# The first pair of heads in larger pieces, turned by TensorE, in a hash-attention and feed-forward kernel

## The chip, the cores and the metric

The kernel runs on one core of a Trainium2 chip. Times are device microseconds (us) of one execution. The granted clock is the share of its full clock that TensorE was allowed at a time. PE is TensorE's matmuls, PEld its weight loads, DVE VectorE, ACT ScalarE, POOL GpSimd and SP SyncE. A "q" behind an engine's name is that engine's instruction queue, which also issues transfers.

## The reference

```python
# q, k, v: (4, 8, 768, 64); proj: (64, 6); w_in: (512, 2048); w_out: (2048, 512); fp32
q_bits = einsum(q, proj) > 0;  k_bits = einsum(k, proj) > 0     # 6 bits per row
mask   = bucket(q_bits) == bucket(k_bits)
attn   = softmax(where(mask, q k^T / 8, -1e9)) @ v
x      = attn as (3072, 512)
h      = x @ w_in
out    = (h * sigmoid(1.702 h)) @ w_out
```

The weights arrive in 64-bit form and have to be converted to fp32 on the chip.

## The kernel before

Heads are worked on two at a time, so there are 16 pairs, numbered 0 to 15. A pair has four groups of products on TensorE: scores of three key tiles against half of the queries, then the product with v of the group before. The hash bits enter the scores as one more small product, so equal buckets need no mask. For each pair, k and q are loaded in 32 x 32 blocks and turned by VectorE, hashed by TensorE, compared by VectorE into a tile `f`, and eight small copies bring the rows of `f` to the partitions where the bits are needed:

```python
def hashed(n):
    h = dots[n] = mps.tile([P, HS], F32, tag="m", name="hash")
    for i, x in enumerate("kq"):
        for c in range(2):
            r0 = D * i + 32 * c
            nc.tensor.matmul(h[r0 : r0 + 32, :], pf[x], xts[n, x][:, c * HS : (c + 1) * HS], ...)

def featured(n, queues):
    f = wk.tile([P, HS], BF16, tag="f", name="f", bufs=1)
    nc.vector.tensor_scalar(f, dots.pop(n), above[:, 0:1], weight[:, 0:1], op0=Alu.is_gt, op1=Alu.mult)
    for c in range(2):
        for i, x in enumerate("kq"):
            for j in range(2):
                queues[j].dma_start(out=feats[n % 2][x][...], in_=f[...])      # eight row copies
```

Between these, VectorE converts w_in piece by piece: 12 of its 16 pieces during attention, and four (`LATE = 4`) in the feed-forward part, where product 4 needs sums made from the last of them. The main loop, cut to what the change touches:

```python
fetch(0, "k"); fetch(0, "q", (nc.scalar, nc.gpsimd)); fetch_v(0)
for x in "kq": turn(0, x); measure(0, x); fetch(1, x)
hashed(0); featured(0, (nc.sync, nc.scalar)); begin(0, nc.scalar)
for g in range(len(groups) + 4):                  # groups of pair n, at = 0..3
    scores(n, c, range(kt, kt + GT), g > 0)
    if 4 <= g and groups[g - 4][2]: invert(*groups[g - 4][:2])     # 1 / column sums
    if n < last and at < 2: turn(n + 1, "kq"[at]); measure(n + 1, "kq"[at])
    ...
    if n < last and at == 1:
        hashed(n + 1); featured(n + 1, (nc.sync, nc.sync))
        fetch(n + 2, "k"); fetch(n + 2, "q"); fetch_v(n + 1)
    if 3 <= g ...: total(*groups[g - 3][:2])      # column sums by TensorE ("dn")
    ...                                           # conversion steps at at = 0, 2, 3
```

At the very end stands a branch to code that would redo the work in a safe form. With this data that code never runs.

Of the kernel before, what the change touches and what calls it, by code (L numbers as in the profile page):

```python
# [19 lines left out]
P = 128  # L20
# [18 lines left out]
def kernel(  # L39
# [38 lines left out]
    pb = const.tile([P, P], F32, name="pb")  # L78
    nc.vector.memset(pb, 0.0)
    for j in range(2):  # L80
        nc.scalar.dma_start(out=pb[D * j : D * (j + 1), D * j : D * j + NB], in_=proj)
# [21 lines left out]
    for i, (x, signs) in enumerate((("k", (-1.0, 1.0)), ("q", (1.0, -1.0)))):  # L103
        w = pf[x] = const.tile([P, 32], F32, name=f"pf_{x}")
        nc.vector.memset(w, 0.0)
        nc.vector.memset(weight[D * i : D * (i + 1)], FEAT[x])
        for j in range(2):
            rows = slice(D * j, D * (j + 1))
            for h, sign in enumerate(signs):
                c0 = NB * (2 * j + h)  # L110
                nc.vector.tensor_scalar(w[rows, c0 : c0 + NB], pb[rows, D * j : D * j + NB], sign, None, op0=Alu.mult)
        for c in range(2):
            r0 = D * i + 32 * c
            for f in reversed(range(4)):
                nc.vector.memset(above[r0 : r0 + NB * (f + 1)], 0.0 if signs[f % 2] > 0 else -NORMAL)

# [52 lines left out]
    LATE = 4  # L169
# [43 lines left out]
    def prepare(wk, mps, tiles, scale, out_of):  # L213
# [31 lines left out]
    def attention(ff):  # L245
# [4 lines left out]
        with actx:  # L250
# [22 lines left out]
            def fetch(n, name, queues=(nc.sync, nc.sync)):  # L273

                b, hp = pairs[n]
                x = raws[n, name] = ld.tile([P, S // 32, 32], F32, tag=name, name=name)
                src = {"k": k, "q": q}[name]
                for j in range(2):
                    rows = src[b, 2 * hp + j].rearrange("(s p) (a i) -> a p s i", p=32, i=32)
                    for a in range(D // 32):  # L280
                        r0 = D * j + 32 * a
                        queues[j].dma_start(out=x[r0 : r0 + 32], in_=rows[a])

            def fetch_v(n):
                b, hp = pairs[n]
                x = vts[n] = ld.tile([P, T, 2, D], F32, tag="v", name="v", bufs=2)
                for j in range(2):
                    nc.sync.dma_start(out=x[:, :, j, :], in_=v[b, 2 * hp + j].rearrange("(t p) d -> p t d", p=P))
# [24 lines left out]
            def featured(n, queues):  # L313
                f = wk.tile([P, HS], BF16, tag="f", name="f", bufs=1)
                nc.vector.tensor_scalar(f, dots.pop(n), above[:, 0:1], weight[:, 0:1], op0=Alu.is_gt, op1=Alu.mult)
                for c in range(2):
                    for i, x in enumerate("kq"):
                        for j in range(2):
                            r0 = D * i + 32 * c + 2 * NB * j
                            queues[j].dma_start(out=feats[n % 2][x][D * j : D * j + 2 * NB, c * HS : (c + 1) * HS],  # L320
                                                in_=f[r0 : r0 + 2 * NB, :])

            def scores(n, c, kts, bits_first):
                qT, kT, qf, kf = xts[n, "q"], xts[n, "k"], feats[n % 2]["q"], feats[n % 2]["k"]
                cols = slice(c * HS, (c + 1) * HS)
                ps = [sps.tile([P, 2, 512], F32, tag="s", name="ps") for _ in kts]

                dot, bits = (kT, qT), (kf, qf)
                todo = [(p, kt, x) for x in ((bits, dot),) for p, kt in zip(ps, kts)] if bits_first else \
                    [(p, kt, (x,)) for x in (dot, bits) for p, kt in zip(ps, kts)]  # L330
                for p, kt, xs in todo:
                    keys = slice(kt * P, (kt + 1) * P)
                    for x in xs:
                        for j in range(2):
                            hs = slice(D * j, D * (j + 1))
                            first = x is (bits if bits_first else dot)
                            nc.tensor.matmul(p[:, j, 0:HS], x[0][hs, keys], x[1][hs, cols], start=first, stop=not first)  # L337
                for p, kt in zip(ps, kts):
                    nc.scalar.activation(es[c][:, kt, :, 0:HS], p[:, :, 0:HS], Act.Exp, scale=1.0 / D**0.5)  # L339
# [65 lines left out]
            def begin(n, *args):  # L405
                if n < min(len(in_chunks) - LATE, last + 1):
                    conv[n] = convert(cv, *in_chunks[n], *args)
# [13 lines left out]
            fetch(0, "k")  # L421
            fetch(0, "q", (nc.scalar, nc.gpsimd))
            fetch_v(0)
            for x in "kq":
                turn(0, x)
                measure(0, x)
                if last:
                    fetch(1, x)
            hashed(0)
            featured(0, (nc.sync, nc.scalar))  # L430
            begin(0, nc.scalar)
            for g in range(len(groups) + 4):
                n, c, kt = groups[g] if g < len(groups) else (last + 1, 0, 0)
                at = 2 * c + kt // GT
                if n <= last:
                    scores(n, c, range(kt, kt + GT), g > 0)
                if 4 <= g and groups[g - 4][2]:
                    invert(*groups[g - 4][:2])
                if n < last and at < 2:
                    turn(n + 1, "kq"[at])  # L440
                    measure(n + 1, "kq"[at])
                if 4 <= g and groups[g - 4][2]:
                    norm(*groups[g - 4][:2])
# [5 lines left out]
                if n < last and at == 1:  # L449
                    hashed(n + 1)  # L450
                    featured(n + 1, (nc.sync, nc.sync))
# [4 lines left out]
                if 3 <= g <= len(groups) + 2 and groups[g - 3][2]:  # L456
                    total(*groups[g - 3][:2])
                if n == last and at in (1, 3):
                    guard(at // 2)
                if at == 0:  # L460
                    step(n)
                elif at == 2:
                    step(n, 2)
                    if n > last - len(x_sums):
                        x_sums[n - last - 1]()
# [3 lines left out]
                if g == len(groups):  # L469
                    for f in in_sums(0):  # L470
                        f()
                    early.close()
# [3 lines left out]
    def shifted_attention():  # L476
# [3 lines left out]
        with actx:  # L480
# [48 lines left out]

            for n, (b, hp) in enumerate(pairs):  # L530
                tiles, ready = load(ld, n, 1), {}
                for f in prepare(wk, mps, tiles, -1.0 / D**0.5, ready):
# [14 lines left out]
    def feed_forward(tag, late=()):  # L547
# [4 lines left out]
        with ExitStack() as fctx:  # L552
# [105 lines left out]
            for sb in range(n1):  # L658
                for mt in range(FC // 2):
                    n = sb * (FC // 2) + mt  # L660
                    if n == 1:
# [7 lines left out]
                        todo += [lambda: [next(steps) for _ in range(2 * LATE // 2)]] * 2 if late else []  # L669
# [74 lines left out]
```

## Time and profile before

| | before |
|---|---|
| time, median of 6 runs with the result | 945.08 us (944.55 to 945.32) |
| span of the profile | 943.7 us |
| PE busy | 916.0 us, 97% |
| PE waits before 22 us | 15.4 us |
| PE waits at the passage to the feed-forward part | 1.4 and 2.5 us |
| end of the last vector operation to the end of the span | 7.5 us |

With an engine at 97%, the busy shares say only that little can be won. The list of what that engine waits for says where. The prediction below shows the lines.

### The profile page before, as it was taken

To read this page: it belongs to the slowest core of one execution; us is meant where nothing else is said; L and a number is where in the kernel's file an instruction comes from. 1 tells how busy PE (TensorE), PEld (TensorE's weight loads), DVE (VectorE), ACT (ScalarE), POOL (GpSimd) and SP (SyncE) were. 2 spreads that over 40 slices of the span, in tenths; PEclk is the share of its full clock that TensorE was granted. 3 is DMA by queue.
4 is the path that set the end of the run, shared out by engine and by line. 5 is a ranking of instruction groups with operands and counts; after the bars stand their busy time and mean duration, and the time that the engine had idled before them with its cause. 6 is when DMAs were issued, how large, how long until landed. Compare 5 with 4: busy or idle time off the path is not lost.

```text
span 943.7 us, 11414 instructions
## 1 busy us (share of the span) xinstructions
PE 916.0 (97%) x4193; PEld 527.6 (56%) x4193; DVE 566.8 (60%) x785; ACT 300.2 (32%) x481; POOL 160.9 (17%) x114
## 2 busy tenths in 40 slices
PE   3999999999999999989999999999999999999996
PEld 1444444444444444434444444447888888888885
DVE  3689999899877655797877787435222313141410
ACT  1666666666666642223233323221000000000000
POOL 2422332332243361050001000500000000000000
PEclk9999999999999999999999999999999999999999
DMA  8434345443333101343333383228242415130101
GB/s 119 82 78 80 78 85 103 96 92 80 77 56 66 39 23 73 128 156 135 133 134 131 124 305 132 90 89 267 93 131 74 149 62 162 56 123 12 34 11 37
DMA packets 177185, 94.30 MB, mean 100 GB/s; under 512 B 128416, under 2 KB 160672, under 8 KB 177120
## 3 DMA queue, kind: packets, MB, share of 16 engines
q1 hardware_dynamic: 175056, 92.53, 34.9%
q10 hardware_dynamic: 1968, 0.76, 0.4%
q8 instruction: 35, 0.57, 0.3%
q0 software_dynamic: 96, 0.20, 0.1%
q14 instruction: 30, 0.25, 0.1%
HBM read 60.82 MB, written 31.46 MB: 98 GB/s over the span
## 4 chain that ended last, share of the span: by engine, by line
PE 56%; DVE 1%; DMA 0%; POOL 0%; issue 0%; DVEq 0%; SPq 0%
PE product L638 31%; PE product L596 25%; DMA raw<-in_moe_w_in_dram 0%; DVE w_in_sb L156 0%; DVE bits L149 0%; DVE c L580 0%; DVE sign L152 0%; DVE sign L146 0%; POOL s_in L173 0%; POOL w_in_sb L174 0%; DVE w_in_sb L161 0%; DVE w_in_sb L158 0%; DVE c L569 0%; DVE bits L147 0%; POOL s_in L175 0%
## 5 line engine op out<-in xcount | busy, mean ns | idle before, releaser
L339 ACT ACTIVATE e<-ps 128x768 f32<-128x768 f32 x192 | 153.3, 812 | 99.4 <-PE ps L337 97.7
L337 PE MATMUL ps<-qT,kT 64*128 64x384 f32 x768 | 157.4, 490 | 0.0
L362 PE MATMUL av<-e,v 128*64 128x385 f32 x768 | 138.4, 495 | 0.0
L596 PE MATMUL product<-xT,w_in_sb 128*128 128x512 f32 x288 | 135.6, 593 | 0.0
L600 ACT ACTIVATE c<-c 128x512 f32<-128x512 f32 x72 | 45.2, 630 | 174.5 <-DVE c L571 126.2
L567 ACT COPY u<-product 128x512 f32<-128x512 f32 x30 | 17.3, 577 | 248.1 <-PE product L638 242.0
L596 PE MATMUL product<-t_x,s_in 128*128 128x512 f32 x192 | 92.0, 602 | 2.5 <-POOL s_in L175 2.5
L362 PEld LDWEIGHTS av<-e,v 128*64 128x64 f32 x768 | 49.3, 136 | 80.6 <-issue 79.9
L348 POOL TENSOR_TENSOR acc<-e 128x768 f32<-128x768 f32 x32 | 55.8, 1743 | 224.1 <-DVE acc L354 179.5
L596 PEld LDWEIGHTS product<-xT,w_in_sb 128*128 128x128 f32 x288 | 54.7, 191 | 69.7 <-issue 62.1
L337 PEld LDWEIGHTS ps<-qT,kT 64*128 64x128 f32 x768 | 69.6, 192 | 31.1 <-issue 31.1
L568 DVE TENSOR_TENSOR v<-product,u 128x512 f32<-128x512 f32 x30 | 20.6, 687 | 86.9 <-PE product L638 72.3
L337 PE MATMUL ps<-qf,kf 64*128 64x384 bf16 x384 | 63.8, 331 | 5.5 <-DMA qf<-f 5.3
L596 PEld LDWEIGHTS product<-t_x,s_in 128*128 128x128 f32 x192 | 36.8, 192 | 49.3 <-issue 45.5
L638 PE MATMUL product<-w_out_sb,xT 128*128 128x256 f32 x288 | 63.6, 379 | 0.0
L638 PE MATMUL product<-w_out_sb,w_in_sb 128*128 128x256 f32 x288 | 63.6, 379 | 0.0
L638 PE MATMUL product<-t_out,xT 128*128 128x256 f32 x288 | 63.6, 379 | 0.0
L638 PEld LDWEIGHTS product<-w_out_sb,xT 128*128 128x128 f32 x288 | 54.7, 190 | 7.9 <-issue 0.5
L638 PEld LDWEIGHTS product<-w_out_sb,w_in_sb 128*128 128x128 f32 x288 | 54.7, 190 | 7.4
L638 PEld LDWEIGHTS product<-t_out,xT 128*128 128x128 f32 x288 | 54.7, 190 | 7.4
L349 POOL TENSOR_TENSOR acc<-acc,e 128x768 f32<-128x768 f32 x32 | 55.1, 1721 | 2.5
L337 PEld LDWEIGHTS <-kf 64*128 64x128 bf16 x384 | 19.0, 95 | 61.3 <-issue 38.0
(104 smaller groups left out, 1108.1 us busy)
## 6 DMA issues: line engine op xcount, KB each, us to landing
g_dram<-c SPq DMA_DIRECT2D x72, 256.0 KB
xT<-g_dram SPq DMA_DIRECT2D x12, 1024.0 KB
w_in_sb<-g_dram SPq DMA_DIRECT2D x12, 1024.0 KB
raw<-in_moe_w_out_dram SPq DMA_DIRECT2D x16, 512.0 KB
raw<-in_moe_w_in_dram SPq DMA_DIRECT2D x15, 512.0 KB
k<-in_k_dram SPq DMA_DIRECT2D x64, 96.0 KB
v<-in_v_dram SPq DMA_DIRECT2D x32, 192.0 KB
g_dram<-u SPq DMA_DIRECT2D x24, 256.0 KB
```

The source lines that it names most:

```text
L337: nc.tensor.matmul(p[:, j, 0:HS], x[0][hs, keys], x[1][hs, cols], start=first, stop=not first)
L339: nc.scalar.activation(es[c][:, kt, :, 0:HS], p[:, :, 0:HS], Act.Exp, scale=1.0 / D**0.5)
L348: nc.gpsimd.tensor_tensor(acc, e[0], e[1], op=Alu.add)
L349: nc.gpsimd.tensor_tensor(acc, acc, e[2], op=Alu.add)
L362: nc.tensor.matmul(av[D * j : D * (j + 1), :], vt[:, t, j, :], es[c][:, t, j, :], start=(t == 0), stop=(t == T - 1))
L567: nc.scalar.copy(u, product(1))
L568: nc.vector.tensor_tensor(v, product(6), u, op=Alu.add)
L596: nc.tensor.matmul(ps, wq[LEFT[i]][:, kc, :], xq[RIGHT[i]][:, kc, :], start=(kc == 0), stop=(kc == K2 - 1))
L600: nc.scalar.activation(c, c, Act.Gelu_apprx_sigmoid)
L638: nc.tensor.matmul(ps[:, m, :], x[:, m * P : (m + 1) * P], wqs[RIGHT[i]][:, c, :], start=(c == 0), stop=(c == FC // 2 - 1))
```

## The change

Its intent is to start TensorE earlier. k and q of the first pair come in 256-byte packets. TensorE turns them, in six transposes each, and makes their hashes with the bits already on the rows where they are needed, so pair 0 has no row copies. The turning of pair 1 moves one group later (`turns = at - (n == 0)`). Conversion starts one pair later and runs to pair 14, so two pieces are left for the end instead of four. The last inversion moves ahead of the first vector work of the feed-forward part. The diff, cut to its core:

```diff
+            def first_pair():
+                for name, src, order, queue in (("k", k, "(p t) d -> p t d", nc.sync), ("q", q, "(t p) d -> p t d", nc.scalar)):
+                    x = ld.tile([P, T, 2, D], F32, tag=name, name=name)
+                    for j in range(2):
+                        queue.dma_start(out=x[:, :, j, :], in_=src[b, 2 * hp + j].rearrange(order, p=P))
+                for name, move in (("k", nc.vector.tensor_copy), ("q", nc.scalar.copy)):
...
+                        nc.tensor.transpose(tp[:, c, i * P : (i + 1) * P], x[:, t], ident)
+                    move(xt.rearrange("p (c s) -> p c s", c=2), tp[:, :, 0:HS])
+                for c in range(2):
+                    for name in "kq":
+                        nc.tensor.matmul(h, pf0[name]..., xts[0, name][:, cols], start=True, stop=True)
+                        nc.vector.tensor_scalar(feats[0][name][:, cols], h, above0[name][:, 0:1], FEAT[name], ...)
...
-    LATE = 4
+    LATE = 2
...
-                if n < min(len(in_chunks) - LATE, last + 1):
-                    conv[n] = convert(cv, *in_chunks[n], *args)
+                if n - 1 < len(in_chunks) - LATE:
+                    conv[n] = convert(cv, *in_chunks[n - 1], nc.sync if n > 1 else nc.scalar)
...
+                turns = at - (n == 0)
-                if n < last and at < 2:
-                    turn(n + 1, "kq"[at])
+                if n < last and 0 <= turns < 2:
+                    turn(n + 1, "kq"[turns])
...
+                elif at == 1 and n > last - len(x_sums):
+                    x_sums[n - last - 1]()
...
                 if g == len(groups):
                     for f in in_sums(0):
                         f()
+                    invert(*started[g + 1])
+                    norm(*started.pop(g + 1))
```

The products for pair 0's dot parts, which before were made ahead of the bits, now follow the bits like everybody else's.

More of the change, by code (lines that the diff above doesn't have):

```diff
@@ L75 @@
     nc.scalar.activation(const.tile([1, 1], F32, name="first"), ones[0:1, 0:1], Act.Exp)
-    pb = const.tile([P, P], F32, name="pb")
-    nc.vector.memset(pb, 0.0)
+    pj = const.tile([P, NB], F32, name="pj")
     for j in range(2):
-        nc.scalar.dma_start(out=pb[D * j : D * (j + 1), D * j : D * j + NB], in_=proj)
+        nc.scalar.dma_start(out=pj[D * j : D * (j + 1)], in_=proj)
     def offsets(name, row):
@@ L110 @@
                 c0 = NB * (2 * j + h)
-                nc.vector.tensor_scalar(w[rows, c0 : c0 + NB], pb[rows, D * j : D * j + NB], sign, None, op0=Alu.mult)
+                nc.vector.tensor_scalar(w[rows, c0 : c0 + NB], pj[rows], sign, None, op0=Alu.mult)
         for c in range(2):
@@ L115 @@
                 nc.vector.memset(above[r0 : r0 + NB * (f + 1)], 0.0 if signs[f % 2] > 0 else -NORMAL)
+    pf0 = {x: const.tile([P, 2, D], F32, name=f"pf0_{x}") for x in "kq"}
+    above0 = {x: const.tile([P, 1], F32, name=f"above0_{x}") for x in "kq"}
+    for i, x in enumerate("kq"):
+        nc.gpsimd.memset(pf0[x], 0.0)
+        nc.gpsimd.memset(above0[x], 0.0)
+        for j in range(2):
+            nc.gpsimd.tensor_copy(pf0[x][:, j, 0 : 2 * NB], pf[x][:, 2 * NB * j : 2 * NB * (j + 1)])
+            nc.gpsimd.tensor_copy(above0[x][D * j : D * j + 2 * NB], above[D * i : D * i + 2 * NB])
     xT = const.tile([P, KC, N], F32, name="xT")
@@ L211, in load, with prepare @@
         return tiles
-    def prepare(wk, mps, tiles, scale, out_of):
+    def prepare(wk, mps, pb, tiles, scale, out_of):
         steps = []
@@ L271, in attention, with fetch @@
             raws, vts, xts = {}, {}, {}
-            def fetch(n, name, queues=(nc.sync, nc.sync)):
+            def fetch(n, name):
                 b, hp = pairs[n]
@@ L281, in fetch @@
                         r0 = D * j + 32 * a
-                        queues[j].dma_start(out=x[r0 : r0 + 32], in_=rows[a])
+                        nc.sync.dma_start(out=x[r0 : r0 + 32], in_=rows[a])
             def fetch_v(n):
@@ L287, in fetch_v @@
                 for j in range(2):
-                    nc.sync.dma_start(out=x[:, :, j, :], in_=v[b, 2 * hp + j].rearrange("(t p) d -> p t d", p=P))
+                    order = "(t p) d -> p t d" if n else "(p t) d -> p t d"
+                    nc.sync.dma_start(out=x[:, :, j, :], in_=v[b, 2 * hp + j].rearrange(order, p=P))
+            def first_pair():
+                b, hp = pairs[0]
+                for name, src, order, queue in (("k", k, "(p t) d -> p t d", nc.sync), ("q", q, "(t p) d -> p t d", nc.scalar)):
+                    x = ld.tile([P, T, 2, D], F32, tag=name, name=name)
+                    raws[0, name] = x.rearrange("p t j d -> p (t j) d")
+                    for j in range(2):
+                        queue.dma_start(out=x[:, :, j, :], in_=src[b, 2 * hp + j].rearrange(order, p=P))
+                for name, move in (("k", nc.vector.tensor_copy), ("q", nc.scalar.copy)):
+                    x = raws[0, name].rearrange("p (t j) d -> p t (j d)", j=2)
+                    xt = xts[0, name] = wk.tile([P, S], F32, tag=f"{name}T", name=f"{name}T")
+                    tp = sps.tile([P, 2, 512], F32, tag="s", name="tp")
+                    for t in range(T):
+                        c, i = divmod(t, GT)
+                        nc.tensor.transpose(tp[:, c, i * P : (i + 1) * P], x[:, t], ident)
+                    move(xt.rearrange("p (c s) -> p c s", c=2), tp[:, :, 0:HS])
+                    measure(0, name)
+                for c in range(2):
+                    cols = slice(c * HS, (c + 1) * HS)
+                    for name in "kq":
+                        h = sps.tile([P, 2, 512], F32, tag="s", name="hash0")[:, 0, 0:HS]
+                        nc.tensor.matmul(h, pf0[name].rearrange("p j d -> p (j d)"), xts[0, name][:, cols], start=True, stop=True)
+                        nc.vector.tensor_scalar(feats[0][name][:, cols], h, above0[name][:, 0:1], FEAT[name],
+                                                op0=Alu.is_gt, op1=Alu.mult)
             def turn(n, name):
@@ L311, in hashed, with featured @@
                                          start=True, stop=True)
-            def featured(n, queues):
+            def featured(n):
                 f = wk.tile([P, HS], BF16, tag="f", name="f", bufs=1)
@@ L319, in featured, with scores @@
                             r0 = D * i + 32 * c + 2 * NB * j
-                            queues[j].dma_start(out=feats[n % 2][x][D * j : D * j + 2 * NB, c * HS : (c + 1) * HS],
+                            nc.sync.dma_start(out=feats[n % 2][x][D * j : D * j + 2 * NB, c * HS : (c + 1) * HS],
                                                 in_=f[r0 : r0 + 2 * NB, :])
-            def scores(n, c, kts, bits_first):
+            def scores(n, c, kts):
                 qT, kT, qf, kf = xts[n, "q"], xts[n, "k"], feats[n % 2]["q"], feats[n % 2]["k"]
                 cols = slice(c * HS, (c + 1) * HS)
-                ps = [sps.tile([P, 2, 512], F32, tag="s", name="ps") for _ in kts]
-                dot, bits = (kT, qT), (kf, qf)
-                todo = [(p, kt, x) for x in ((bits, dot),) for p, kt in zip(ps, kts)] if bits_first else \
-                    [(p, kt, (x,)) for x in (dot, bits) for p, kt in zip(ps, kts)]
-                for p, kt, xs in todo:
+                for kt in kts:
+                    ps = sps.tile([P, 2, 512], F32, tag="s", name="ps")
                     keys = slice(kt * P, (kt + 1) * P)
-                    for x in xs:
+                    for a, m, last in ((kf, qf, False), (kT, qT, True)):
                         for j in range(2):
                             hs = slice(D * j, D * (j + 1))
-                            first = x is (bits if bits_first else dot)
-                            nc.tensor.matmul(p[:, j, 0:HS], x[0][hs, keys], x[1][hs, cols], start=first, stop=not first)
-                for p, kt in zip(ps, kts):
-                    nc.scalar.activation(es[c][:, kt, :, 0:HS], p[:, :, 0:HS], Act.Exp, scale=1.0 / D**0.5)
+                            nc.tensor.matmul(ps[:, j, 0:HS], a[hs, keys], m[hs, cols], start=not last, stop=last)
+                    nc.scalar.activation(es[c][:, kt, :, 0:HS], ps[:, :, 0:HS], Act.Exp, scale=1.0 / D**0.5)
             accs, avs = {}, {}
@@ L403, in step, with begin @@
                     next(conv.get(n, iter(())), None)
-            def begin(n, *args):
-                if n < min(len(in_chunks) - LATE, last + 1):
-                    conv[n] = convert(cv, *in_chunks[n], *args)
+            def begin(n):
+                if n - 1 < len(in_chunks) - LATE:
+                    conv[n] = convert(cv, *in_chunks[n - 1], nc.sync if n > 1 else nc.scalar)
                     step(n)
@@ L419, in guard @@
                     nc.vector.tensor_reduce(largest[0:1, 0:1], row, axis=AX.X, op=Alu.max)
-            fetch(0, "k")
-            fetch(0, "q", (nc.scalar, nc.gpsimd))
+            started = {}
+            first_pair()
             fetch_v(0)
             for x in "kq":
-                turn(0, x)
-                measure(0, x)
-                if last:
-                    fetch(1, x)
-            hashed(0)
-            featured(0, (nc.sync, nc.scalar))
-            begin(0, nc.scalar)
+                fetch(1, x)
             for g in range(len(groups) + 4):
@@ L435, in attention @@
                 if n <= last:
-                    scores(n, c, range(kt, kt + GT), g > 0)
-                if 4 <= g and groups[g - 4][2]:
-                    invert(*groups[g - 4][:2])
-                if n < last and at < 2:
-                    turn(n + 1, "kq"[at])
-                    measure(n + 1, "kq"[at])
-                if 4 <= g and groups[g - 4][2]:
-                    norm(*groups[g - 4][:2])
+                    scores(n, c, range(kt, kt + GT))
+                turns = at - (n == 0)
+                if g in started:
+                    invert(*started[g])
+                if n < last and 0 <= turns < 2:
+                    turn(n + 1, "kq"[turns])
+                    measure(n + 1, "kq"[turns])
+                if g in started:
+                    norm(*started.pop(g))
                 if 1 <= g <= len(groups):
@@ L448, in attention @@
                         unload(*groups[g - 1][:2])
-                if n < last and at == 1:
+                if n < last and turns == 1:
                     hashed(n + 1)
-                    featured(n + 1, (nc.sync, nc.sync))
+                    featured(n + 1)
                     for x in "kq":
@@ L457, in attention @@
                     total(*groups[g - 3][:2])
+                    started[g + 1] = groups[g - 3][:2]
                 if n == last and at in (1, 3):
@@ L461, in attention @@
                     step(n)
+                elif at == 1 and n > last - len(x_sums):
+                    x_sums[n - last - 1]()
                 elif at == 2:
                     step(n, 2)
-                    if n > last - len(x_sums):
-                        x_sums[n - last - 1]()
                 elif at == 3:
@@ L528, in turn @@
                             nc.vector.tensor_copy(dst, tp)
+            pb = st.tile([P, P], F32, name="pb", bufs=1)
+            nc.vector.memset(pb, 0.0)
+            for j in range(2):
+                nc.vector.tensor_copy(pb[D * j : D * (j + 1), D * j : D * j + NB], pj[D * j : D * (j + 1)])
             for n, (b, hp) in enumerate(pairs):
                 tiles, ready = load(ld, n, 1), {}
-                for f in prepare(wk, mps, tiles, -1.0 / D**0.5, ready):
+                for f in prepare(wk, mps, pb, tiles, -1.0 / D**0.5, ready):
                     f()
@@ L668, in feed_forward @@
                         steps = conversions(cv, late + [(w_out_sb[:, :, fc, :], wo[fc]) for fc in range(FC)])
-                        todo += [lambda: [next(steps) for _ in range(2 * LATE // 2)]] * 2 if late else []
+                        todo += [lambda: [next(steps) for _ in range(LATE)]] * 2 if late else []
                         todo += [lambda: (next(steps), next(steps))] * FC
```

## The prediction

> **What bounds the kernel now.** I read the page first, for the busy shares:
>
> ```profile
> PE 916.0 (97%) x4193; PEld 527.6 (56%) x4193; DVE 566.8 (60%) x785; ACT 300.2 (32%) x481; POOL 160.9 (17%) x114
> ```
>
> TensorE (PE) is busy for 916.0 of 943.7 us. A change that leaves its matmuls alone can only win from the other 27.7 us, or from matmuls that run slowly. So the next view is the list of PE's waits:
>
> ```profile
> PE hash L310 <- DVE kT L293: 7.7, 1, 7.7
> PE ps L337 <- DMA qf<-f: 5.3, 1, 5.3
> PE product L596 <- POOL s_in L175: 2.5, 1, 2.5
> PE hash L310 <- DVE qT L293: 2.4, 1, 2.4
> PE dn L380 <- DVE rt L387: 1.4, 1, 1.4
> PE ps L337 <- ACT e L339: 0.3, 1, 0.3
> ```
>
> These are all: 19.6 us. The rest is the end: PE's last matmul ends at 935.5 and the last vector operation and store follow, about 8 us, which the change does not touch. Of the 19.6, 15.4 are before 22 us, 1.4 and 2.5 at the passage from attention to the feed-forward part. The order of time shows where:
>
> ```profile
> 7.73 1.50 PE L310 MATMUL hash<-kT,pf_k 128*32 128x384 f32 x4 [7.73 <-DVE kT L293]
> 10.62 0.98 DVE L293 STREAM_TRANSPOSE qT<-q 128x768 f32<-128x768 f32 x1 [2.94 <-DMA q<-in_q_dram]
> 13.07 3.55 PE L337 MATMUL ps<-qT,kT 64*128 64x384 f32 x12
> 21.89 1.15 PE L337 MATMUL ps<-qf,kf 64*128 64x384 bf16 x6 [5.27 <-DMA qf<-f]
> ...
> 27.18 2.16 PE L362 MATMUL av<-e,v 128*64 128x385 f32 x12
> ...
> 363.53 0.87 PE L380 MATMUL dn<-acc,ones 128*64 128x384 f32 x4 [1.36 <-DVE rt L387]
> ...
> 401.78 0.69 DVE L161 SCALAR_TENSOR_TENSOR w_in_sb<-size,w_in_sb 128x512 f32<-128x512 f32 x1
> ...
> 404.81 3.68 PE L596 MATMUL product<-t_x,s_in 128*128 128x512 f32 x4 [2.46 <-POOL s_in L175]
> 408.29 1.92 PE L596 MATMUL product<-xT,w_in_sb 128*128 128x512 f32 x4
> ```
>
> At the start: q lands at 10.6, the hashes go through VectorE and eight small copies onto their rows, and only at 21.9 can PE go on. The first value product, at 27.18, is my mark; from there PE is never idle until 362. At 404.8 PE waits for sums made from the last converted piece of w_in, whose conversion ends at 402.5.
>
> [...]after 404.81 four matmul pieces take until 408.29, 3.48 us, where the same four start 1.72 apart when warm; from 21.89 to about 26 the granted clock is 0.50.[...] 128-byte packets of k and q moved at 213 GB/s at best (2.5 to 3.0 us, 859 packets), 256-byte ones of v at 257 (61.0 to 61.5, 512 packets)[...] Here a copy of hash rows issued at 19.59 releases PE at 21.89: 2.3 us.
>
> **Part 1, the start.** k and q now come in four issues of 192 KB with 256-byte packets; none is on GpSimd's queue, whose issues took 5.2 us to land. Before, data of both queues moved about in order of issue (the scalar queue's second q piece, issued at 2.53, moved at 5.0 to 5.5, after all of k). The new order: k in two, proj, v and q interleaved, then v of the next pair. q is complete after 3 x 1536 packets at 1024 per us (512 in 0.5 us), 4.5 us from the first packet at 1.8: 6.3, say 6.6. From k's last packet to its use was 1.6 us (5.0 to 6.6), so q is there at about 8.2.
> - Six transposes. Cold weight loads take 0.34 us each (warm 0.19), so an estimated 2.4: 10.7. The copy on ScalarE (like an exp of 768, 0.81) runs beside the first hash.
> - Four hash products in a row, all ahead of the scores in PE's order. A cold pair of 32-column hashes took 1.50 for four pieces at 7.73; two pieces of 128 x 384, run alone, should take 1.28 cold, 0.64 warm. Four cold: 5.1, so 15.8; if the clock comes up on the way, 14. VectorE's evictions (0.68 each, as L315's) fit between; no copy to other rows is left. I take 15.3 for the first score.
> - Two groups of scores at 2.45 (three times 0.82 at 30 us) bring the first value product to 20.2 against 27.18. The dot products made ahead at 13.07 are lost, which this counting has inside. **Gain 7.0.**
>
> **Part 2, pair 1 shifted by one group.** Its hash moves one group closer to its use. In the trace, from the hash's end at 30.1 the fourth row copy, issued at 33.3, lands 2.3 later: 5.5 after the hash, where PE then has one group, 4.6 us. **Loss 0.9.** In the built order the last of pair 2's four pieces of k moved behind all eight row copies: issue about 7.1 after the hash, landing 2.9 later (estimate), at 10. From that turn of k to the end of the turn of q, VectorE took 7.7 us before (39.67 to 47.3), of which 1.3 was waiting beside GpSimd. The next hash is due 15.5 after, so PE waits 1 to 2. **Loss 1.3.**
>
> **Part 3, conversion one pair later, two pieces fewer at the end.** Fourteen of sixteen pieces are now converted in attention, in pairs 1 to 14, where pairs 12 to 14 had none; the four 1.22 us sums of x fall in pairs 12 to 15 too. VectorE, by stretches of 19.97 us, has 18.0 to 18.9 busy in a conversion pair; with a sum it is full. But it idles 1.1 to 1.8 us per pair for the raw piece (at 229.6 and 250.9), whose issue sits behind other loads on the queue, so the sum should fall into that gap. With a little lateness: **loss 0.6.** In the feed-forward part each of two slots converts one piece instead of two: the last one ends near 396 instead of 402.5 and its sums by 399, before PE needs them at 402.4. That frees the 2.46 and the half-clock stretch after it (3.48 - 1.72 = 1.76): **gain 4.2.**
>
> **Part 4, the last inversion.** The reciprocal of the last pair's first half now stands ahead of the feed-forward's vector work, so the second half's total finds its buffer free. **Gain 1.4**, and 0.1 of slower pieces after it.
>
> **Sum.** 7.0 - 0.9 - 1.3 - 0.6 + 4.2 + 1.5 = 9.9. 945.1 - 9.9 = 935.2, rounded 935.
>
> **Rivals.**
> 1. *The start is hidden anyway, or given back.* For: PE still starts cold and has twelve transposes more; four hashes are serial; q's landing depends on v, queued between. If q lands at 10 and all stays cold, the start gains 5, and with 3 us of stall in pair 1 the total is 6: 939. Against: 5.3 us of waiting for row copies is gone whatever the loads do.
> 2. *VectorE becomes the bound in pairs 12 to 14.* For: 18.9 of 19.97 plus 1.22. Turn of q and hash are already 0.07 us apart there (254.79, 254.85), so lateness goes straight to PE. Three pairs at 1.3 would cost 4 more than I count, also 939. Against: the raw wait.
> 3. *All fits.* Transposes warm the clock after all, the stalls of part 2 vanish in the queue's slack: first score at 13.5, no losses: 9 + 5.7 = about 14.5, 930.5.
> 4. *The late conversion was not the last thing that held product 4.* The chain of waits goes through it step by step from 388 to 404.8, so I give this little: without that gain, 939.
>
> **Range and chances.** The passage (5.7) rests on measured waits; the start (5 to 9) and the new stalls (0.5 to 5) are worked out. Both bad ends together give 940, both good 930; 8 in 10 lies in 930.5 to 939.5. Faster by over 2% needs 926.2, 18.9 us, nearly all the idle time there is before the tail: 0.03. Slower by 2% needs 19 us of new stalls in an otherwise full PE: 0.01.
>
> **What would show it.** PE's waits without s_in L175 and without rt L387; the first value product near 20; q's copy near 10.7; a wait of about 1 us for a row copy at pair 1 and one for the turn of q at pair 2; no wait of PE from 40 us to the end of attention longer than 0.5. Wrong would be: a first value product after 23, a PE wait in pairs 12 to 14 over 1 us, or a wait at product 4 that stays.

## The result, and the profile after

The changed kernel took 936.78 us (median of 6 runs, 935.9 to 937.59) against 945.08. Ratios in this document are the mean time of one kernel's fast runs over that of the other's of the same rounds, so not quite the ratio of the medians that are quoted. Here the ratio is 0.9912, interval 0.9899 to 0.9925: 8.3 us less, "within 2%", and inside the range. The predicted time was 935.0.

First the page's busy shares of the changed kernel:

```profile
PE 915.0 (98%) x4205; PEld 529.6 (57%) x4205; DVE 567.0 (61%) x786; ACT 301.8 (32%) x482; POOL 159.4 (17%) x124
```

Nothing in the amount of work moved: the twelve more TensorE instructions are the twelve transposes. The waits of PE (us in total, times, longest):

```profile
PE tp L315 <- POOL above_q L124: 7.2, 1, 7.2
PE ps L368 <- DMA qf<-f: 2.0, 1, 2.0
PE tp L315 <- DMA q<-in_q_dram: 0.5, 1, 0.5
PE hash L346 <- DVE qT L329: 0.4, 1, 0.4
```

The first is the wait for k: the name given is the semaphore that the profile dates last, but the transposes start when ScalarE starts on k, both at 7.1 us. The waits for `s_in` and for `rt` are gone. Two small ones are new, and the timeline shows them in their places (start, duration, engine, line, operation, and in brackets the idle time before it with its releaser):

```profile
9.15 1.51 PE L315 MATMUL tp<-ident,q 128*128 128x128 f32 x6 [0.48 <-DMA q<-in_q_dram]
...
10.46 1.48 PE L322 MATMUL hash<-kT,pf_k 128*128 128x384 f32 x2
11.74 1.30 PE L322 MATMUL hash<-qT,pf_q 128*128 128x384 f32 x2
12.88 0.81 PE L322 MATMUL hash<-kT,pf_k 128*128 128x384 f32 x2
13.53 0.81 PE L322 MATMUL hash<-qT,pf_q 128*128 128x384 f32 x2
...
19.21 2.16 PE L392 MATMUL av<-e,v 128*64 128x385 f32 x12
...
29.63 0.35 ACTq L144 DMA_DIRECT2D raw<-in_moe_w_in_dram  x1
...
33.42 0.40 PE L368 MATMUL ps<-qf,kf 64*128 64x384 bf16 x2 [2.02 <-DMA qf<-f]
...
34.03 0.51 SPq L291 DMA_DIRECT2D k<-in_k_dram  x1
...
43.57 0.84 PE L346 MATMUL hash<-kT,pf_k 128*32 128x384 f32 x4
44.76 0.84 PE L346 MATMUL hash<-qT,pf_q 128*32 128x384 f32 x4 [0.35 <-DVE qT L329]
...
357.61 0.87 PE L410 MATMUL dn<-acc,ones 128*64 128x384 f32 x4
...
386.85 0.69 DVE L170 SCALAR_TENSOR_TENSOR w_in_sb<-size,w_in_sb 128x512 f32<-128x512 f32 x1
...
389.11 0.73 POOL L184 TENSOR_TENSOR s_in<-s_in,w_in_sb 128x256 f32<-128x256 f32 x1
...
396.27 1.88 PE L632 MATMUL product<-t_x,s_in 128*128 128x512 f32 x4
```

Of the clock at the start, the views by stretches print 1.00, but the trace holds no record of it before 12.69 us, where the first one, of the full clock, begins. That TensorE was at half clock until then is read from the durations: the hashes of 10.46 and 11.74 start 1.28 us apart, those of 12.88 and 13.53 only 0.65.

The first value product comes at 19.21 instead of 27.18, which is 7.97 us earlier. By the first feed-forward product, 4.49 are left (349.88 against 345.39). At pair 1, PE waits 2.0 us for a row copy. At pair 2 the hashes of k and q, which stand side by side in a later pair, come one after the other. From the value product before them to the scores after them it is 4.25 us (41.28 to 45.53) instead of 2.87 (47.09 to 49.96 before), so this costs 1.4 us, of which the wait shown is 0.35. The passage to the feed-forward part gives 5.85 more: `dn` follows without a wait. The last conversion ends at 387.5 and GpSimd's sums from it at 389.8, 6.4 us before the product that needs them (396.27, the one that waited until 404.81 before). PE's last product ends 10.35 us earlier than before.

But the span is only 8.3 us shorter. From the end of the last vector operation to the end of the span it was 7.5 us before (943.7 less 936.20) and is 9.5 after (935.4 less 925.86). Apart from the last store, which has been moved by 929 us in the changed kernel, only fetches of instructions move in that time. The queue's line of the view of transfers, of the last eight or nine us (packets, MB, share), is for the kernel before:

```profile
q14 instruction: 4, 0.03, 1.8%
```

and for the changed kernel:

```profile
q14 instruction: 5, 0.04, 1.8%
```

One fetch more; five make 0.04 MB, so each is of 8 KB. The starts of SyncE's last instructions, in ns from one to the next, after its last branch, show where it falls:

```
before: 2722, 78, 64, 67, 59, 62, 59, 62, ...
after:  2766, 81, 2197, 83, 64, 66, 60, 61, ...
```

These are the semaphore waits that close the program; they start some 70 ns apart (59 to 83). In the changed kernel SyncE stands still for 2.2 us between the second and the third, from 931.98 to 934.18, and one of the five fetches, of 8192 bytes, moves in that time, from 932.70 to 933.01. In both kernels 2.7 us pass after the branch, and two of the fetches move in them (from 940.11 to 940.98 before, from 929.79 to 930.60 after). That SyncE waits for the fetch in the 2.2 us, because its closing instructions lie in two of the 8192-byte pieces, is theory, which a run below tests.

### The profile page after: what moved, and what is told of

Read it like the earlier page. It is cut to its first block, busy times and chain, and to the rows that moved or that the text cites. A ratio compares the mean times of both kernels' runs of the same rounds, so it can differ in the third digit from the quotient of the medians.

```text
span 935.4 us, 11429 instructions
## 1 busy us (share of the span) xinstructions
PE 915.0 (98%) x4205; PEld 529.6 (57%) x4205; DVE 567.0 (61%) x786; ACT 301.8 (32%) x482; POOL 159.4 (17%) x124
## 4 chain that ended last, share of the span: by engine, by line
PE 96%; DMA 1%; DVE 1%; SPq 1%; issue 0%; ACTq 0%; ACT 0%; DVEq 0%
PE product L674 31%; PE product L632 31%; PE ps L368 16%; PE av L392 14%; PE dn L410 2%; PE hash L346 1%; DMA q<-in_q_dram 1%; SPq L356 1%; PE hash L322 0%; DMA k<-in_k_dram 0%; DVE bits L156 0%; PE tp L315 0%; DVE qT L329 0%; DVE kT L329 0%; DVE acc L383 0%
## 5 line engine op out<-in xcount | busy, mean ns | idle before, releaser
L368 PE MATMUL ps<-qT,kT 64*128 64x384 f32 x768 | 155.2, 482 | 0.0
L607 DVE TENSOR_TENSOR c<-product,c 128x512 f32<-128x512 f32 x30 | 20.7, 691 | 53.6 <-PE product L674 37.3
```

The source lines that it names most:

```text
L368: nc.tensor.matmul(ps[:, j, 0:HS], a[hs, keys], m[hs, cols], start=not last, stop=last)
L607: nc.vector.tensor_tensor(c22, p, c21, op=Alu.add)
```

## The experiments

All were correct and ran for five rounds beside the kernel before, whose medians in these rounds were 944.8 to 946.3. So a difference of less than about 1 us between medians of different rounds is not settled by the times alone. Each edit is one of the changed kernel.

### The first raw piece on SyncE's queue

```diff
-                    conv[n] = convert(cv, *in_chunks[n - 1], nc.sync if n > 1 else nc.scalar)
+                    conv[n] = convert(cv, *in_chunks[n - 1], nc.sync)
```

> Only the first raw piece of w_in is issued on the sync queue (there early, before pair 1's k) instead of the scalar queue at 29.6 us, where its 512 KB moved between 30.5 and 32.9 and pair 1's row copies stood still. Theory A (the wait of 2.0 us for the row copies is all that the raw piece costs, and it adds to the rest): that wait falls to about 0.9 and the last matmul ends 1.1 us earlier than in the changed kernel. Rival B (behind it stands a second chain, row copies issued until 34.0, then the fourth piece of pair 2's k, then VectorE until the turn of q at 44.7): the first wait falls to 0.9, but the wait for the turn of q grows from 0.35 to about 1.4 and the end moves by less than 0.3 us.

The question is why the row copies of pair 1 took 2.0 us of waiting where 0.9 was predicted. In the changed kernel, from 27 to 37 us, ScalarE's queue moved the first raw piece of w_in (packets, MB, share) among the row copies:

```profile
q10 hardware_dynamic: 144, 0.52, 15.9%
```

With the raw piece early on SyncE's queue, ahead of pair 1's loads, that line is gone and the wait for rows is 0.4 us. But the time is 936.63 us (ratio 0.9905, the changed kernel's was 0.9912): nothing gained. The lines of this run say why:

```profile
43.71 0.84 PE L346 MATMUL hash<-kT,pf_k 128*32 128x384 f32 x4 [1.54 <-DVE rt L417]
44.91 0.84 PE L346 MATMUL hash<-qT,pf_q 128*32 128x384 f32 x4 [0.35 <-DVE qT L329]
```

The hash of pair 2 comes at the same place, 43.7, whether PE waits before it or at it. Its chain is the other one: the last piece of pair 2's k stands behind eight row copies on the queue (issued at 34.14 here, 34.03 in the changed kernel), then come VectorE's turn of k, its work of that group, and the turn of q. The two losses were two waits on one chain. (This profile is of the slowest of the four runs. It lost another 0.9 us at the hash of pair 14, at 291.84, where a raw piece came late to VectorE and the hash was split in the same way.)

### The shift of pair 1 undone

```diff
-                turns = at - (n == 0)
+                turns = at
```

> Only the shift of pair 1's turns, hash and row copies by one group is undone; the start, the conversion's shift and the rest stay. Theory (the shift costs 3.3 us: a wait of 2.0 for row copies and 1.2 at the next hash, and pair 1's k and q land by 17 us, early enough for the old place): both waits vanish and the last matmul ends 3.3 us earlier, about 921.9. Rival (k and q of pair 1 land too late for the old place, which is why it was shifted): a new wait of 1 to 3 us at the first hash, and no gain.

This took 934.0 us (933.81 to 934.47, ratio 0.9881), 2.8 less than the changed kernel. k and q of pair 1 are there in time (VectorE turns them at 14.5 and 16.5), and the wait for row copies is gone from PE's list. The split hash of pair 2 is still there:

```profile
40.43 0.84 PE L346 MATMUL hash<-kT,pf_k 128*32 128x384 f32 x4
41.62 0.84 PE L346 MATMUL hash<-qT,pf_q 128*32 128x384 f32 x4 [0.35 <-DVE qT L329]
```

So the shift bought nothing at the start and cost the 2.0 us. Of the 3.3 us expected, the 1.2 at the next hash did not come. PE's last product ended at 922.1, close to the 921.9 expected, only because the start, which the edit does not touch, was 0.95 us quicker in this profile.

### Also k of pair 2 ahead of the row copies

```diff
-                turns = at - (n == 0)
+                turns = at
...
+                    if n + 2 <= last:
+                        fetch(n + 2, "k")
                     featured(n + 1)
-                    for x in "kq":
-                        if n + 2 <= last:
-                            fetch(n + 2, x)
+                    if n + 2 <= last:
+                        fetch(n + 2, "q")
```

> The changed kernel with the shift of pair 1 undone (which gave 934.0 us) and all four loads of the third pair's k issued ahead of the row copies of the second. In the run with the shift undone the last two of these loads stood behind the row copies, k landed at 33.9 us and the hash of the third pair came in two parts, 1.2 us later than one. Theory: k lands before 25 us, the hash of the third pair comes in one piece, the end of the last vector operation is 1.0 to 1.3 us earlier, 932.8 us. Rival 1: the row copies are issued later behind the loads and the first score of the second pair waits for them (0.5 to 1.5 us), 934 us. Rival 2: q of the third pair, still behind the row copies, sets the time of the hash by itself, 934 us.

VectorE now turns that k at 28.47 instead of 33.89 us (it had landed by then and VectorE was held by the scores that read the tile it writes, so when it landed isn't seen), and the hash of pair 2 is one piece again, k and q side by side:

```profile
40.32 0.52 PE L346 MATMUL hash<-kT,pf_k 128*32 128x384 f32 x2
40.34 0.52 PE L346 MATMUL hash<-qT,pf_q 128*32 128x384 f32 x2
40.67 0.49 PE L346 MATMUL hash<-kT,pf_k 128*32 128x384 f32 x2
40.68 0.49 PE L346 MATMUL hash<-qT,pf_q 128*32 128x384 f32 x2
```

PE waits for nothing after q's landing. The last vector operation of the profiled run ended at 921.7 against 922.8 of the run above, 1.1 earlier, as expected. The time is 933.71 us (ratio 0.9877 against 0.9881): the times alone don't resolve it.

### Four late conversions again

```diff
-    LATE = 2
+    LATE = 4
```

> Only the number of pieces of w_in left for the feed-forward part goes back from two to four; the start and the early inversion stay. Theory: the wait for s_in and the stretch at half clock after it come back, 2.5 + 1.8 = 4.2 us, last matmul at about 929.4. Rival (part of that gain came from the shorter vector work elsewhere, or pairs 12 to 14 pay for their conversions): less than 3 us later.

939.49 us (938.98 to 941.86, ratio 0.9946), 2.7 more than the changed kernel. The wait is back:

```profile
397.93 1.98 PE L632 MATMUL product<-t_x,s_in 128*128 128x512 f32 x4 [2.31 <-POOL s_in L184]
399.75 1.88 PE L632 MATMUL product<-xT,w_in_sb 128*128 128x512 f32 x4
```

The half-clock stretch that followed it in the kernel before is not: the next four start 1.82 later, not 3.48. The two slowest of the five runs, 940.44 and 941.86, have a mean clock of 0.994 where the profiled one has 0.996, so in those the stretch may have come; no trace of them was taken. The wait cost 2.31 us in this profile, and in that of the kernel before 4.2 with the slow stretch (2.46 and 1.76).

### The last inversion back in its place

```diff
                 if g == len(groups):
                     for f in in_sums(0):
                         f()
-                    invert(*started[g + 1])
-                    norm(*started.pop(g + 1))
```

> The changed kernel with the early last inversion undone: the last column sums are inverted one task later, as before. Theory (the step of the prediction): the first vector work of the next stage waits again for the inversion, so the wait of TensorE for the first dn product, 1.4 us before the change, is back, the first feed-forward product comes 1.4 to 1.5 us later, and the kernel takes 938.2 us (the changed kernel 936.8). Rival: with the late conversion shorter the queue of VectorE is empty there anyway, no wait, 936.8 us.

937.95 us (ratio 0.9919), 1.2 more than the changed kernel by the medians and 0.7 by the ratios, close to the 938.2 expected, with the wait of before to a hundredth:

```profile
360.16 0.87 PE L410 MATMUL dn<-acc,ones 128*64 128x384 f32 x4 [1.36 <-DVE rt L417]
```

This profiled run was its slowest, 939.39 (the others 937.72 to 938.01), and shows what the wait for row copies at 34 us can do. Of the view by stretches (from and to, length, PE, PEld, DVE, ACT and POOL busy, granted clock, DMA share, GB/s), this run:

```profile
36.00:40.00 4.00, 4.00 (x21) 1.93 (x20) 2.20 (x3) 2.81 (x4) 0.00 (x0) 0.75 0.74 118
```

and the changed kernel's:

```profile
36.00:40.00 4.00, 4.00 (x28) 1.88 (x28) 2.78 (x3) 2.72 (x7) 0.00 (x0) 1.00 0.81 130
```

After a wait of 2.16 us the clock was at 0.50 from 34.58 to 37.99, so 0.75 on average here, and PE did 21 matmuls where it does 28 at the full clock. After the 2.02 us of the changed kernel it did not fall (1.00 from 33 to 40 us). Other waits went both ways too: after the 2.46 us of the kernel before, at product 4, it was at 0.50 from 404.94 to 408.36; after the 2.31 us of the run with four late conversions it stayed at 1.00 (395 to 408.3).

### Warming the clock: matmuls, and transposes

```diff
+                warm = sps.tile([P, 2, 512], F32, tag="s", name="warm")
+                for i in range(18):
+                    nc.tensor.matmul(warm[:, 0, 0:P], ident, ident, start=True, stop=True)
```

> Eighteen matmuls of the identity with itself are put ahead of the first transposes, where TensorE waits idle for k until 7.1 us; nothing else. Theory (the first hashes run at half clock because TensorE was idle): with TensorE busy from about 1.5 us on, the first two hash products take 0.64 instead of 1.3 us each and the first score starts 1 to 1.5 us earlier, the end likewise. Rival (the evictions and the arrival of q set the start, or the clock has fallen again by 9 us since the matmuls end near 7): less than 0.4 us.

```diff
+                for i in range(22):
+                    nc.tensor.transpose(warm[:, 0, 0:P], ident, ident)
```

> The changed kernel with 22 transposes of the identity on TensorE, from 1.5 us on, ahead of the first pair's turns (the earlier run with 18 matmuls there had the turns in 0.85 us and the hashes in 0.8 to 0.9 us instead of 1.51 and 1.3 to 1.5 us). Theory A: transposes do not count as work for the clock, so turns take 1.5 us, the first hash 1.5 us as in the changed kernel, first score at 14.3 us after the start. Theory B: they count like matmuls, turns 0.85 us, hashes 0.8 to 0.9 us, first score 13.0 to 13.6 us. The time of the whole kernel 936.2 to 937.2 us in either, since the run with matmuls gave the same time as the changed kernel.

Both stand ahead of the first turns. With matmuls:

```profile
9.58 0.85 PE L318 MATMUL tp<-ident,q 128*128 128x128 f32 x6 [1.06 <-DMA q<-in_q_dram]
10.26 0.81 PE L325 MATMUL hash<-kT,pf_k 128*128 128x384 f32 x2
11.40 0.88 PE L325 MATMUL hash<-qT,pf_q 128*128 128x384 f32 x2 [0.33 <-ACT qT L319]
```

With transposes:

```profile
8.77 0.85 PE L318 MATMUL tp<-ident,q 128*128 128x128 f32 x6 [1.30 <-DMA q<-in_q_dram]
9.45 0.81 PE L325 MATMUL hash<-kT,pf_k 128*128 128x384 f32 x2
10.60 0.88 PE L325 MATMUL hash<-qT,pf_q 128*128 128x384 f32 x2 [0.33 <-ACT qT L319]
```

The turns of q take 0.85 instead of 1.51 us and the first hashes 0.81 and 0.88 instead of 1.48 and 1.30, in both. The first record of the full clock begins at 5.92 us with the matmuls and at 6.09 with the transposes, when TensorE had done nothing but these transposes. So the 22 transposes brought the clock up as the 18 matmuls did. The times, 937.12 (ratio 0.9909) and 936.2 us (0.9906), are hardly different from the changed kernel's. In the profiles, the first value product came 0.75 and 1.56 us earlier than there. The waits for row copies stayed (1.5 and 1.6 us), and waits for `rt` (1.1 and 0.7 us) and split hashes at pairs 2 and 3 took the gain back: with matmuls all of it (PE's last product 0.98 later), with transposes half (0.78 earlier).

### The projection's loads on GpSimd's queue

```diff
-        nc.scalar.dma_start(out=pj[D * j : D * (j + 1)], in_=proj)
+        nc.gpsimd.dma_start(out=pj[D * j : D * (j + 1)], in_=proj)
```

> The changed kernel with the two small loads of the projection moved from the queue ahead of q's two loads to GpSimd's queue, so that q's first piece is issued at 0.7 us instead of 2.0. Theory: q lands at 7.9 to 8.4 us instead of 9.1, the turns of q follow those of k (which end near 8.7) nearly at once, the first score comes 0.4 to 1.0 us earlier (14.3 us in the changed kernel), and the time falls by as much unless it is given back at pair 1's row copies, where a wait of 2.0 us stands: 936 to 936.8 us. Rival: k, q and v share the same 16 DMA engines, so q lands when the bytes ahead of it are through and not 1.3 us earlier, or k lands later by as much; first score at 14.2 us or later, 936.8 us.

A miss of both theories: 939.06 us (ratio 0.9923), slower by 2.3 by the medians and by 1.0 by the ratios.

```profile
8.00 1.49 PE L315 MATMUL tp<-ident,q 128*128 128x128 f32 x6
10.71 1.65 PE L322 MATMUL hash<-kT,pf_k 128*128 128x384 f32 x2 [1.22 <-POOL pf_k L123]
```

q is there before the turns of k are done, so 1.15 us are won there. But the projection now comes late, the hash waits 1.22 us for its weights, and the clock stays low longer: three of the four hashes took 1.48 to 1.65 us. The wait at pair 1 was 2.28 us and was followed by a stretch of low clock (0.67 from 36 to 40 us). The first value product came at 20.43, 1.2 later than in the changed kernel. How much of this is the later projection and how much the clock, which varies from run to run, is not shown.

### SyncE's last instructions moved

```diff
         whole(feed_forward("2"))
+        with tc.tile_pool(name="pad", bufs=1) as pad:
+            x = pad.tile([P, 8], F32, name="pad")
+            for i in range(8):
+                nc.sync.dma_start(out=x[:, i : i + 1], in_=v[0, 0, 0:P, i : i + 1])
```

> The changed kernel with eight small loads added on SyncE's queue at the end of the branch that never runs, so that nothing executed changes but the place of SyncE's last instructions. The trace of the changed kernel shows a gap of 2.2 us between the second and the third of the semaphore waits with which SyncE ends, and a fifth fetch of 8 KB of instructions in it; the kernel before has no gap there. Theory (the end of SyncE's program straddles two fetched blocks of instructions): the gap goes, the time from the end of the last vector operation to the end falls from 9.5 to 7.3 to 7.6 us, the kernel takes 934.6 us. Rival (the longer tail comes from the last store or from the memory): it stays at 9.5 us and 936.8 us.

These loads stand in the branch that never runs, so nothing that executes has changed. The gap is gone, SyncE's last starts are 2649, 78, 64, 67, 59 ns apart, and the line of instruction fetches at the end has four packets again:

```profile
q14 instruction: 4, 0.03, 1.4%
```

From the last vector operation's end to the end: 7.4 us, against 9.5. The time is 935.19 us (934.46 to 936.37, ratio 0.9895), 1.6 less than the changed kernel. Fetch and stand-still went together, as the theory expected, and the rival (the store or the memory) falls. The other profiles agree: in all nine of the changed kernel and its versions without the eight loads there are five such fetches in the last 9 us and 9.2 to 9.6 us at the end, in the three versions with the loads four fetches and 7.4 to 7.8 us.

### All of it together

The shift undone, k of pair 2 ahead of the row copies, the 22 transposes, the projection on GpSimd's queue and the eight loads:

> The version that the runs so far point to: the changed kernel with the shift of pair 1 undone, k of the third pair loaded ahead of the row copies, 22 transposes of the identity ahead of the first turns, the projection's loads on GpSimd's queue, and the eight loads in the branch that never runs, which move the end of SyncE's program. If the gains add up: 933.7 (shift undone and k ahead) less 1.2 (clock up at the first turns) less 0.4 to 1.0 (q earlier) less 2.1 (no fetch within SyncE's last instructions) is 929.4 to 930.0 us. Rival: the gain of the start is given back in a wait for row copies or loads of the next pairs, as in the earlier run with warm matmuls, and only the tail's 2.1 remains: 931.6 us. Either beats both kernels.

930.48 us (930.38 to 930.67, ratio 0.9839), between the two expectations. The tail is 7.8 us and PE, once it has its first score, waits for nothing more. One wait stood at the start: the first hash waited 1.10 us for a weight tile, whose copy on GpSimd stood behind clearings of the bit tiles. In a last version VectorE makes these copies:

```diff
-            nc.gpsimd.tensor_copy(pf0[x][:, j, 0 : 2 * NB], pf[x][:, 2 * NB * j : 2 * NB * (j + 1)])
+            nc.vector.tensor_copy(pf0[x][:, j, 0 : 2 * NB], pf[x][:, 2 * NB * j : 2 * NB * (j + 1)])
```

> The best version so far (930.5 us) with the four small copies that make the first hashes' weights on VectorE instead of GpSimd. In that run the last of them stood on GpSimd behind clearings of the bit tiles until 9.4 us and the first hash waited 1.1 us for it, while VectorE had nothing to do from 7.3 to 7.9 us. Theory: the wait goes, the hash of k starts when kT is copied (8.9 us), the first score comes 0.6 to 0.8 us earlier than 12.6 us, and the time is 929.8 us. Rival: the copy of qT on ScalarE (9.4 us) and the loads of the next pair set the start by themselves, 930.3 us or more.

929.71 us (929.29 to 929.88, ratio 0.9824), as expected. The full list of PE's waits is now

```profile
PE warm L311 <- POOL ident masks.py:199: 2.4, 1, 2.4
PE hash L325 <- DVE kT L319: 1.1, 1, 1.1
```

and the first score starts at 11.94 us, against 14.27 in the changed kernel, the first value product at 16.89 against 19.21. The hash still waits for VectorE, now for the copy of kT itself, at 9.19 and not at 8.9. This version beats both kernels. It also shows that the gain of a warm start is kept once the row copies don't hold pair 1. Its parts were not all run one by one, and how much of it is the projection's new place is not known.

## Why the prediction was right or wrong

The class, the range and the signs of most steps were right. The sizes, from the profiled runs:

| step | predicted | measured |
|---|---|---|
| start, at the first value product | 7.0 | 7.97 |
| row copies of pair 1 | -0.9 | -2.16 |
| hash of pair 2 | -1.3 | -1.38 |
| pairs 12 to 14 | -0.6 | 0 |
| up to the first feed-forward product | 4.2 | 4.49 |
| late conversion and last inversion | 5.7 | 5.85 |
| up to PE's last product | 9.9 | 10.35 |
| the tail, "which the change does not touch" | 0 | -2.0 |
| total | 9.9 | 8.3 |

The losses of pairs 1 and 2 are taken between value products: the lead is 7.97 us at the first, 5.81 after pair 1's first scores (41.82 against 36.01) and 4.43 after pair 2's (52.49 against 48.06).

- **The start** was mis-sized in three terms that went against each other. q landed at 9.1 instead of 8.2, the six transposes took 1.51 instead of 2.4, and the four hashes were half cold, half warm (starts 1.28 and 0.65 us apart): the clock was up at 12.9, and the first score came at 14.27 instead of 15.3. That the copy of q stands at 10.70, where 10.7 was predicted, is luck: two errors of 0.9 us cancelled. How early the clock comes up varies from run to run: where the start was not edited, the first record of the full clock begins between 10.7 and 14.1 us in the profiles, and the first value product came between 18.3 and 19.8. This step took transposes to do nothing for the clock, which no trace had shown. The run with 22 of them ahead shows that they brought it up (turns of q in 0.85 instead of 1.51 us).
- **The row copies of pair 1.** The mechanism (the fourth row copy lands after the only group there is to hide it) was right and the term of 0.9 was mis-sized. The wait was 2.0 (with slower pieces after it 2.16), because the first raw piece was issued on the other queue in the middle of the row copies, as the run with that piece moved shows (0.4 without it).
- **The hash of pair 2** was right in size. But the two losses were added as though each could be won alone. Freeing the row copies only moved the wait to the hash. The chain through the queue was the cause of both, and undoing the shift removed the first, reordering k the second.
- **Pairs 12 to 14** lost nothing: their hashes are 20.55 us apart in both kernels (229.79, 250.35, 270.90 after). The 0.6 for lateness was not needed in this profile, and rival 2 did not come true in it. But the profile of the run with the raw piece moved lost 0.9 us at pair 14, so such lateness can happen. The prediction's stretches of 19.97 us were also a little short: pairs are 20.55 apart in its own trace too, which leaves VectorE 0.6 us more than it counted.
- **The late conversion and the last inversion** were right, and each was shown by its own undoing, 2.7 and 1.2 us. Their 3.9 is less than the 5.7 because 1.76 of the latter was the half-clock stretch, which the profile of the kernel before had after a wait of 2.46 us, and that of the run with four late conversions did not have after one of 2.31. Rival 4 fell.
- **The step that failed**, and that took the gain from 10.35 us at PE's last product to 8.3 in all, is "the last vector operation and store follow, about 8 us, which the change does not touch". The change lengthens or shortens programs, in the branch that never runs too, and with it came a fifth fetch at the end and SyncE's stand-still of 2.2 us: the tail is 2.0 us longer. Eight loads in that branch took both away (7.4 us of tail). Without that, the prediction of the total would have been 0.4 us too cautious instead of 1.6 too bold.
- **Rival 1** (the start is given back) was partly true, in a form that it did not name: not a late q or a cold TensorE, but a chain through the queue that begins when the hash of pair 1 is made. Rival 3 (all fits, 930.5) is nearly what the best version reached, after the shift was undone.

## What to carry to other kernels

When two waits follow each other on an otherwise full engine, look for one chain behind both before adding their lengths: removing one alone may only move the time to the other (here the wait for rows fell from 2.0 to 0.4 us, and the time was 936.63 against 936.78). A small transfer that the critical engine needs should not share its moment with a large one from another queue (2.0 us of wait for the row copies with the raw piece among them, 0.4 without), and loads that are needed soon belong ahead of a run of small copies (k of pair 2 was turned at 28.47 instead of 33.89 us). When spans differ by about 2 us and every engine's work ends as it should, compare the very end of the program: a stand-still among its closing instructions was worth 2.0 us here, as much as many a tuning step, and an edit of code that never runs took it away (1.6 us in the median, 2.1 in the tail).
